# Early score maxima of ten query tiles: tile 0 and tiles 4 to 9 folded, and PSUM banks closed to maxima ahead of transposes and products

## The chip, the cores and the metric

One core of a Trainium2 chip runs the whole program in one launch. The metric is device time in microseconds (us), lower is better. TensorE is called PE, VectorE DVE, ScalarE ACT, GpSimd POOL and SyncE SP, as in the profile. L12 is line 12 of the kernel before, unless "of the change" stands beside it.

## The reference, cut to what matters

```python
for _ in range(2):                               # x is 2048 x 512
    n = layernorm(x)
    x = x + Cr @ (n @ Dr.T) - Ci @ (n @ Di.T)    # DFT over the sequence (2048) and over D (512)
    n = layernorm(x)
    q, k, v = n @ wq, n @ wk, n @ wv             # 32 query heads, one k and one v head, Dh = 16
    p = softmax(q @ k.T * 16 ** -0.5)            # for every head, 2048 x 2048
    x = x + (p @ v) @ wo
```

Everything is fp32 in and out. The softmax needs the maximum of each row of scores before the exponentials, and it is these maxima that the change moves.

## The kernel before, in words

Each of the two layers has a first phase (the Fourier part, then q, k and v) and a second phase (attention). The 2048 positions are 16 tiles of 128. Products run in fp32r, with operands split into a high and a low part, so a product of full accuracy is three matmuls. The DFT products from row 48 on, the scores and the maxima use 64 of PE's 128 rows (64*128 in the profile), and two of them run side by side on the two halves.

**First phase.** A loop over `n` from 0 to 127, called rows here, with 32 rows for each group of four tiles. A row of the first 112 multiplies one chunk of the DFT matrix into PSUM tiles `x` (L87 to L89 before row 48, L772 from then on); two rows share one turn of `z_rows`, and a place such as (2, 1) in the task table means quarter 1 of row 2 of a group. At the end of a group come the products with the hidden DFT (`y_rows`, L574), the residual sum (`y_out`, L556) and the statistics of the layer norm. While the next group's rows run, `prep_tasks` prepares the four tiles just finished: root and inverse of the variance (`ln_root`, `ln_inv`), the normalisation (`ln_apply`, L189), a PE transpose of each tile through bank `z` (`tr_tile`, L266), the k and v product (`kv`, L87 to L89 on a `y` bank), the transpose of v, and four q products (`q_mm`, on a `y` bank), whose results go to DRAM.

**Maxima.** A block is one PE matmul of a query tile's head pair with 512 keys (128 x 512 scores in one PSUM bank) and the DVE pass that takes its maximum. One tile has 16 pairs, two halves g and four key blocks, 128 blocks. Blocks of the first phase are *early*: the table `EARLY` lists tile, key block, the slot that holds the tile's queries, the row of its load, the row from which its blocks may be issued, the row by which they must be done, and the number of pairs. `pump` is called between the DFT products and issues a block when the kernel's own clocks (`clk`, a planner inside the recording code) say that a bank is free; `flush(n)`, at the start of row n, issues what is still left of the entries due, without waiting for a free bank and with nothing between. The banks are three `y` and one `z`.

An entry marked "f" is *folded*: the keys of blocks 0 and 1 are taken together. A first matmul with `kd` (block 0's keys less block 1's) gives a difference, ACT writes its Relu to `rel` or `kraw` (L463), a second matmul with `kz` gives block 1's scores, and one DVE pass (L468) adds the two and takes the maximum. So a folded pair of blocks is two matmuls, one ACT pass and one DVE pass; unfolded it is two matmuls and two DVE passes (L473). The `rel` and `kraw` tiles are one buffer for each half.

**Second phase.** 512 steps (16 tiles by 32 steps). A step is four score matmuls into two `x` tiles (L942; some of the last tile's into `y`, L935), two exponentials on ACT (L945, 128 x 1024), and the product of the step before last with v into bank `z` (L956, eight records of PE for a step). The remaining blocks (L398, L399) are issued by `more_max` in the order of the tiles, as many as `owed` allows: three to a step on average, four at most in one. A tile's blocks can be issued only when its queries are loaded (`o.loaded`): tile 13 takes the slot that tile 10's queries leave, so its load stands at step 0 of tile 11 and it counts as loaded at step 4 of tile 11. After each tile comes the output product with wo (12 matmuls).

## Time and profile before

| | us |
|---|---|
| median of 3 runs | 3548.38 (3547.25 to 3548.52) |
| the profiled execution | 3548.28 |
| its span in the profile | 3546.4 |
| first phase, layer 0 and layer 1 | about 0 to 633 and 1776 to 2395 |
| second phase, layer 0 and layer 1 | about 633 to 1776 and 2395 to 3546 |
| early blocks in a layer | 560 |
| blocks of `more_max` in a layer | 1472 |

The span begins with the first recorded instruction; 1.9 us of the execution lie outside it. Rows of a timeline are start, duration, engine, line, operation, written tile and read tiles. Matmuls overlap in the pipeline, so the distance between starts, not the duration, tells what one costs PE. An idle time stands in brackets with what ended it.

### The profile page before, as it was taken

The page shows a single profiled execution, that of the slowest core. Times are in us where ns is not written, and L with a number is a line of the kernel's source. Part 1 is how long each engine was busy: PE and PEld are TensorE (multiplying, and loading weights), DVE is VectorE, ACT ScalarE, POOL GpSimd, SP SyncE. Part 2 cuts the span into 40 slices and gives each one's busy share as a digit, 9 for nine tenths or more (in the row PEclk, how much of TensorE's full clock was granted, in tenths as well). Part 3 has the DMA queues.
Part 4 walks back from the last instruction along what each step waited for, and adds up shares of the span by engine and source line. Part 5 has one row for each costly group of instructions (what it writes and reads, how often), then busy time and mean ns, then how long its engine had stood idle before and what let it go on. Part 6 is the DMA issues. An engine that isn't in the chain of part 4 may idle for free.

```text
span 3546.4 us, 64237 instructions
## 1 busy us (share of the span) xinstructions
PE 3490.2 (98%) x24576; PEld 1884.6 (53%) x24576; DVE 2723.9 (77%) x4905; ACT 2499.3 (70%) x3204; POOL 818.7 (23%) x1212
## 2 busy tenths in 40 slices
PE   8999999999999999999999999999999999999999
PEld 6897879433333333333378978783333333333333
DVE  6267776888888888888432777768888888888883
ACT  4223733888888888888932237438888888888888
POOL 4244342211221122112213443322101110111011
PEclk9999999999999999999999999999999999999999
DMA  6445252311111100111144342423111111011100
GB/s 192 148 145 167 82 163 90 85 52 34 35 37 50 35 23 23 50 34 26 40 143 125 125 146 93 149 71 88 46 38 35 49 34 38 23 35 38 37 23 25
DMA packets 224899, 254.54 MB, mean 72 GB/s; under 512 B 52880, under 2 KB 174800, under 8 KB 217424
## 3 DMA queue, kind: packets, MB, share of 16 engines
q1 hardware_dynamic: 210384, 233.12, 21.5%
q0 software_dynamic: 14208, 17.33, 1.6%
q8 instruction: 193, 3.16, 0.4%
q14 instruction: 114, 0.93, 0.1%
HBM read 187.16 MB, written 65.27 MB: 71 GB/s over the span
## 4 chain that ended last, share of the span: by engine, by line
PE 93%; DVE 4%; ACT 2%; issue 1%; POOL 0%; DMA 0%; SPq 0%; ACTq 0%; DVEq 0%; POOLq 0%
PE z L956 29%; PE x L942 19%; PE y L398 13%; PE x L772 11%; PE y L87 3%; PE y L459 3%; PE y L88 2%; PE y L89 2%; PE x L574 2%; PE x L87 2%; PE x L89 2%; PE x L88 2%; DVE mxe L473 1%; DVE mxp L473 1%; PE z L459 1%
## 5 line engine op out<-in xcount | busy, mean ns | idle before, releaser
L945 ACT ACTIVATE slot<-x 128x1024 f32<-128x1024 f32 x2000 | 1946.2, 1024 | 284.2 <-PE x L942 272.3
L399 DVE TENSOR_REDUCE mxp<-y 128x1 f32<-128x512 f32 x2944 | 1849.8, 684 | 179.4 <-PE y L398 167.2
L956 PE MATMUL z<-slot,v 128*32 128x512 f32 x8192 | 1096.3, 605 | 1.6 <-DVE row L960 0.7
L942 PE MATMUL x<-slot,kz 64*128 64x512 f32 x2976 | 677.9, 451 | 0.7 <-DMA slot<-craw 0.4
L942 PEld LDWEIGHTS x<-slot,kz 64*128 64x128 f32 x2976 | 279.3, 184 | 742.9 <-ACT slot L945 686.4
L398 PE MATMUL y<-kz,slot 64*128 64x512 f32 x2176 | 581.2, 396 | 0.7 <-DVE mxp L399 0.4
L956 PEld LDWEIGHTS z<-slot,v 128*32 128x32 f32 x8192 | 163.4, 108 | 362.1 <-issue 331.1
L772 PE MATMUL x<-cl,xnh 64*128 64x512 f32 (+1 forms) x1536 | 352.4, 353 | 0.0
L772 PE MATMUL x<-ch,xnl 64*128 64x512 f32 (+1 forms) x1536 | 347.4, 358 | 1.1 <-ACT xnl L561 1.0
L772 PE MATMUL x<-ch,xnh 64*128 64x512 f32 (+1 forms) x1536 | 339.0, 358 | 6.5 <-DVE row L556 3.9
L398 PEld LDWEIGHTS y<-kz,slot 64*128 64x128 f32 x2176 | 277.5, 186 | 22.6 <-DVE mxp L399 10.4
L79 POOL TENSOR_TENSOR cl<-craw,ch 128x512 fp32r<-128x512 f32 x176 | 225.1, 1299 | 192.3 <-ACT ch L78 180.5
L78 ACT CAST ch<-craw 128x512 fp32r<-128x512 f32 x256 | 153.5, 622 | 156.2 <-PE x L89 81.7
L527 POOL DMA_DIRECT2D slot<-mt x224 | 111.5, 505 | 585.8 <-PE y L398 493.4
L459 PE MATMUL y<-kz,slot 64*128 64x512 f32 x602 | 232.7, 397 | 2.0 <-DVE kraw L304 1.0
L772 PEld LDWEIGHTS x<-ch,xnh 64*128 64x128 f32 x1536 | 210.0, 185 | 24.6 <-issue 6.6
L772 PEld LDWEIGHTS x<-ch,xnl 64*128 64x128 f32 x1536 | 214.3, 185 | 15.8 <-issue 4.5
L772 PEld LDWEIGHTS x<-cl,xnh 64*128 64x128 f32 x1536 | 217.3, 185 | 8.0
L997 POOL TENSOR_TENSOR row<-row,row 128x256 f32<-128x256 f32 x63 | 46.6, 739 | 700.1 <-DMA row<-rd 699.8
L473 DVE TENSOR_REDUCE mxe<-y 128x1 f32<-128x512 f32 x310 | 194.9, 680 | 14.0 <-PE y L459 14.0
L87 PE MATMUL x<-ch,xnh 128*128 128x512 f32 x384 | 154.3, 402 | 10.3 <-ACT ch L78 9.0
L89 PE MATMUL x<-ch,xnl 128*128 128x512 f32 x384 | 153.2, 399 | 2.0 <-POOL xnl L638 1.8
(197 smaller groups left out, 4173.8 us busy)
## 6 DMA issues: line engine op xcount, KB each, us to landing
craw<-ct_in SPq DMA_DIRECT2D x112, 512.0 KB
slot<-qd SPq DMA_DIRECT2D x44, 1024.0 KB
qd<-row SPq DMA_DIRECT2D x144, 128.0 KB
od<-row SPq DMA_DIRECT2D x252, 64.0 KB
row<-wqd SPq DMA_DIRECT2D x48, 256.0 KB
row<-x_in SPq DMA_DIRECT2D x32, 256.0 KB
mid<-row POOLq DMA_DIRECT2D x32, 256.0 KB, 2.4
craw<-ct_in SPq DMA_DIRECT2D x32, 256.0 KB
```

Source lines behind the costliest of these rows:

```text
L78: nc.scalar.copy(hi, raw)
L79: (eng or nc.vector).tensor_sub(lo, raw, f(hi))
L87: nc.tensor.matmul(ps_, ah, bh, start=start, stop=False)
L89: nc.tensor.matmul(ps_, al, bh, start=False, stop=stop)
L398: nc.tensor.matmul(pm, o.qT[i][gs, pr, :], kz[gs, c0:c0 + n], start=True, stop=True)
L399: nc.vector.reduce_max(to, pm, axis=AX.X)
L459: nc.tensor.matmul(pm, o.qT[i][gs, pr, :], k[gs, c0:c0 + 512], start=True, stop=True)
L473: nc.vector.reduce_max(to, pm, axis=AX.X)
L772: nc.tensor.matmul(z[d], a[gs, s, d * P:(d + 1) * P], b[gs, :], start=first and q < 2 and e == 0, stop=last and q > 1 and e == len(turns) - 1)
L942: nc.tensor.matmul(st["e"][:, g, :], kz[64 * g:64 * g + KR, c * P:(c + 1) * P], o.qT[i][64 * g:64 * g + KR, cp:cp + 4, :], start=True, sto ...
L945: nc.scalar.activation(ptiles[i, s_][:, 2 * w:2 * w + 2, :], st.pop("e"), AF.Exp, scale=DH ** -0.5)
L956: nc.tensor.matmul(a[32 * j:32 * j + 32, :], v1[:, c, :], pt[:, j, :], start=c == 0, stop=c == NT - 1)
```

## The change

The table of early blocks goes from 560 to 640 blocks a layer: tile 0's key blocks 0 and 1 are now folded, tiles 8 and 9 are new and folded, both due at row 119; (2, 1) and (1, 2) are gone. The preparation of four tiles starts earlier and in smaller steps. `hold` keeps maxima off bank `z` before each transpose; `keep` allocates the `y` bank of a coming k, v or q product ahead of it and lets only two more blocks through on `y`. No early block is issued between rows 64 and 70.8 and between 96 and 98.5. Of two tiles in `y_rows`, both sums now come before both statistics. The variance's eps goes through ACT's bias and POOL. At the end of the first phase four of the last eight maxima of tile 0 are issued one product earlier.

```diff
-    (1, 0, 2, 44, 49, 63, 16), (2, 0, 3, 44, 49, 63, 16), (3, 0, 8, 45, 49.5, 66, 16), (0, 0, 0, 64, 66.5, 79, 16),
-    (0, 1, 0, None, 71.5, 79, 16), (3, 1, 8, None, 71.5, 84, 16), (4, "f", 2, 77, 79.5, 95, 16), (5, "f", 3, 77, 79.5, 95, 16),
-    (6, "f", 8, 84, 87, 128, 16), (2, 1, 0, 96, 98, 111, 16), (1, 1, 1, 96, 98, 111, 16), (1, 2, 1, None, 103.5, 111, 8),
-    (7, "f", 2, 107, 109.5, 119, 16), (0, 2, 8, 101, 103.5, 128, 16),
+    (1, 0, 2, 43, 48, 63, 16), (2, 0, 3, 43, 48, 63, 16), (3, 0, 8, 44, 48, 66, 16), (0, "f", 0, 64, 70.8, 79, 16),
+    (3, 1, 8, None, 70.8, 84, 16), (4, "f", 2, 76, 78.5, 95, 16), (5, "f", 3, 76, 78.5, 95, 16), (6, "f", 8, 84, 87, 101, 16),
+    (7, "f", 0, 96, 98.5, 111, 16), (1, 1, 1, 96, 98.5, 111, 16), (0, 2, 8, 101, 103.5, 128, 16),
+    (8, "f", 2, 107, 109.5, 119, 16), (9, "f", 3, 107, 109.5, 119, 16),
...
-        nc.vector.tensor_scalar(v, mv[:, t0:t0 + n, 1], EPS, None, op0=ALU.add)
-        nc.scalar.activation(w, v, AF.Sqrt)
+        nc.scalar.activation(w, mv[:, t0:t0 + n, 1], AF.Sqrt, bias=eps)
+        nc.gpsimd.tensor_scalar(v, mv[:, t0:t0 + n, 1], EPS, None, op0=ALU.add)
...
+        def keep(after):
+            st["pk"], st["kept"] = bank("y"), 3
+            held("y", clk["pe"] + 1.4 + 2.8 + after)
...
-            tag = "z" if clk["z"] <= clk["y"][0] else "y"
+            tag = "z" if clk["z"] <= clk["y"][0] and not st["hold"] else "y"
...
+            if tag == "y" and st.get("kept") == 1:
+                return False
...
-                            y_out(4 * tb + w[e], y[:, e, :], x1[w[e]])
+                            y_add(4 * tb + w[e], y[:, e, :], x1[w[e]])
+                        for e in range(2):
+                            ln_stats(x1[w[e]], 4 * tb + w[e])
...
-            ts[0] = [alloc]
-            ts[1, 1] = [lambda: ln_inv(*st["root"])]
-            ts[2, 0], ts[2, 2] = [ap(0)], [ap(1)]
-            ts[2] = [lambda: tr(0)]
+            ts[0, 0] = [alloc, lambda: root_(0)]
+            ts[0, 2] = [lambda: ln_inv(*roots[0])]
+            ts[1, 1] = [ap(0), lambda: root_(2)]
+            ts[1, 2] = [ap(1), hold]
+            ts[1, 3] = [lambda: ln_inv(*roots[2])]
+            ts[2, 0] = [lambda: tr_(0)]
...
-            ts[6, 0] = [do_kv]
+            ts[4, 3] = [lambda: keep(2.6)]
+            ts[5, 1] = [do_kv]
...
-                ts[7 + g] = [lambda g=g: q_mm(tb, g, *st["xt"])]
+                ts[6 + g, 1] = [lambda: keep(0.9)]
+                ts[6 + g] = [lambda g=g: q_mm(tb, g, *st["xt"])]
...
-            q_rows(14, 0, *xt[1], lambda: None)
+            ticks = iter([0, 0, 0, 0, 1, 1, 1, 1])
+            q_rows(14, 0, *xt[1], lambda: take(mb, next(ticks)))
```

How the instructions move on PE is shown at three places, all in layer 1. The names are the PSUM bank that is written (`x`, `y`, `z`) and the operands; a row ending in x2 or x4 is that many equal matmuls.

The first transpose of the second group of tiles, before (L266, about row 67):

```order
L459 MATMUL y<-kz,slot_23056 128x512
L772 MATMUL x<-ch,xnh 128x512 x2
L459 MATMUL y<-kz,slot_23056 128x512
L772 MATMUL x<-cl,xnh 128x512 x2
L459 MATMUL z<-kz,slot_23056 128x512
L772 MATMUL x<-ch,xnl 128x512 x2
L266 MATMUL z<-ident,row_22480 128x128 x4
```

And of the change (L268 there, about row 66):

```order
L809 MATMUL x<-ch,xnh 128x512 x4
L809 MATMUL x<-cl,xnh 128x512 x2
L809 MATMUL x<-ch,xnl 128x512 x2
L268 MATMUL z<-ident,row_22653 128x128 x4
L809 MATMUL x<-ch,xnh 128x512 x2
```

Before, a block on bank `z` stands three matmuls ahead of the transpose that needs that bank; in the change no block stands anywhere near it.

The end of row 118, where `flush(119)` issues what is left of the entries due at row 119. Before (L459 are the blocks, `kd` the first matmul of a folded pair):

```order
L772 MATMUL x<-ch,xnl 128x256 x2
L459 MATMUL y<-kz,slot_26162 128x512
L459 MATMUL y<-kd,slot_26162 128x512 x2
L459 MATMUL z<-kz,slot_26162 128x512
L459 MATMUL y<-kz,slot_26162 128x512
L772 MATMUL x<-ch,xnl 128x256 x2
```

Of the change (L475), the beginning of the same place; the pattern of its last rows goes on, with no DFT product in it, until 70 blocks have been issued:

```order
L809 MATMUL x<-ch,xnl 128x256 x2
L475 MATMUL y<-kz,slot_26412 128x512 x2
L475 MATMUL y<-kd,slot_26412 128x512
L475 MATMUL z<-kd,slot_26412 128x512
L475 MATMUL y<-kz,slot_26412 128x512 x2
L475 MATMUL y<-kd,slot_26414 128x512
L475 MATMUL z<-kd,slot_26414 128x512
L475 MATMUL y<-kz,slot_26414 128x512 x2
L475 MATMUL y<-kd,slot_26414 128x512
```

So 5 blocks in a row became 70. Runs of the same kind stand at the ends of row 94 (9 blocks before, 21 now), of row 78 (none before, 9 now) and of row 110 (none before, 9 now, these unfolded).

Second phase, steps 334 and after. Before, every step to 487 carries three blocks (L398) among its scores (L942) and its products with v (L956):

```order
L942 MATMUL x<-slot_32910,kz 128x512 x2
L398 MATMUL y<-kz,slot_34495 128x512 x2
L942 MATMUL x<-slot_32910,kz 128x512 x2
L398 MATMUL y<-kz,slot_34495 128x512
L956 MATMUL z<-slot_36349,v_72 32x512 x4
```

Of the change, where steps without a block (the first three rows, step 356) end and step 357 begins (scores are L980, blocks L408, products with v L994):

```order
L980 MATMUL x<-slot_34217,kz 128x512 x4
L994 MATMUL z<-slot_37258,v_72 32x512 x4
L980 MATMUL x<-slot_34217,kz 128x512 x2
L408 MATMUL y<-kz,slot_37212 128x512 x2
L980 MATMUL x<-slot_34217,kz 128x512 x2
L408 MATMUL y<-kz,slot_37212 128x512 x2
L994 MATMUL z<-slot_37271,v_72 32x512 x4
L980 MATMUL x<-slot_34217,kz 128x512 x2
L408 MATMUL y<-kz,slot_37212 128x512 x2
```

In the change steps 0 to 333 carry three blocks as before, steps 334 to 356 none, steps 357 to 425 four, steps 426 to 461 three, and steps 462 to 511 none; before, steps 0 to 488 carry three and the rest none. 80 blocks fewer stand in this phase, and tile 13's, whose turn now comes at step 334, cannot be issued before step 357.

More of the change, by code (lines that the diff above doesn't have):

```diff
@@ L97, in fnet_mqa_kernel @@
     nc.gpsimd.memset(v1[:, :, DH:DH + 1], 1.0)
+    eps = sb.tile([P, 1], F32, name="eps")
+    nc.gpsimd.memset(eps, EPS)
     kone = sb.tile([P, 1], F32, name="kone")
@@ L271, in tr_tile, with kept @@
                 split_ps(v[0], xth, xtl)
+        def keep(after):
+            st["pk"], st["kept"] = bank("y"), 3
+            held("y", clk["pe"] + 1.4 + 2.8 + after)
+        def kept():
+            st["kept"] = 0
+            return st["pk"]
         def kv(t0, n, xth, xtl, vt=None, now=True):
-            pk = bank("y")[:, :n * P]
+            pk = (bank("y") if now else kept())[:, :n * P]
             spend(pe=2.9, act=1.2)
-            held("y", clk["pe"] + 2.5)
+            if now:
+                held("y", clk["pe"] + 2.5)
             for k in range(NK):
@@ L431, in make_layer @@
                 for e, ent in enumerate(EARLY)}
-        st["skew"], st["rel"], st["subs"] = 0, {}, []
+        st["skew"], st["rel"], st["subs"], st["hold"] = 0, {}, [], False
+        roots = {}
         def pump(n, only=None):
@@ L458, in issue @@
             pm = bank(tag)
+            if tag == "y" and st.get("kept"):
+                st["kept"] -= 1
+                assert st["kept"]
             nc.tensor.matmul(pm, o.qT[i][gs, pr, :], k[gs, c0:c0 + 512], start=True, stop=True)
@@ L686, in prep_tasks, with hold, tr_, root_ @@
[L686 removed]
+            def hold():
+                st["hold"] = True
+            def tr_(tt):
+                st["hold"] = False
+                tr(tt)
+            def root_(e):
+                roots[e] = ln_root(4 * tb + e, 2)
+            ts[0, 0] = [alloc, lambda: root_(0)]
[3 more added lines that the diff above has]
+            ts[1, 3] = [lambda: ln_inv(*roots[2])]
@@ new lines, in prep_tasks @@
+            ts[2, 0] = [lambda: tr_(0)]
+            ts[2, 1] = [hold]
+            ts[2, 2] = [ap(2)]
+            ts[2, 3] = [ap(3), lambda: tr_(1)]
+            ts[3, 0] = [hold]
+            ts[3, 1] = [lambda: tr_(2)]
+            ts[3, 2] = [hold]
+            ts[4, 0] = [lambda: tr_(3), lambda: [wq_load(g) for g in range(2)]]
+            ts[4, 3] = [lambda: keep(2.6)]
+            ts[5, 1] = [do_kv]
+            ts[6, 0] = [lambda: (kv_lo(4 * tb, 4), k_diff(tb) if tb < 2 else None), hold]
```

23 lines of the change are left out of this document (9 added, 14 removed).

## The prediction

> **What bounds the kernel now.** I read the page first, then the busy time by stage, then PE's own waits in the first phase.
>
> ```profile
> span 3546.4 us, 64237 instructions
> PE 3490.2 (98%) x24576; PEld 1884.6 (53%) x24576; DVE 2723.9 (77%) x4905; ACT 2499.3 (70%) x3204; POOL 818.7 (23%) x1212
> ```
>
> ```profile
> 1776.00:2395.00 619.00, 601.00 (x4493) 513.63 (x4491) 378.40 (x751) 242.56 (x502) 200.92 (x196) 1.00 0.38 122
> 2395.00:3546.00 1151.00, 1144.25 (x7811) 430.30 (x7810) 961.46 (x1626) 1000.03 (x1085) 137.87 (x258) 1.00 0.14 39
> ```
>
> The second fence is the first and the second phase of layer 1; the columns are the stretch, its length, and the busy time of PE, PEld, DVE, ACT and POOL. PE is the bound: in the first phase it is idle for 18 of 619 us while DVE works 378. But in the second phase DVE (961 of 1151) and ACT (1000) stand close behind, so what is taken from PE there is worth less than its PE time. Who holds PE up in layer 1's first phase:
>
> ```profile
> PE z L266 <- DVE mxp L473: 3.4, 3, 2.0
> PE z L266 <- DVE mxe L473: 2.7, 3, 1.4
> PE x L772 <- DVE row L556: 1.9, 2, 1.0
> PE y L87 <- DVE mxe L473: 1.4, 3, 0.5
> PE y L87 <- DVE mxp L473: 0.9, 2, 0.5
> PE y L459 <- DVE kraw L304: 0.5, 1, 0.5
> PE z L459 <- ACT v L314: 0.3, 1, 0.3
> ```
>
> Six transposes (L266) and five q products (L87) wait for a DVE maximum in the bank they need. That is what `hold` and `keep` go for. Each wait also costs a restart, which the timeline shows:
>
> ```profile
> 2040.32 0.61 PE L772 MATMUL x<-ch,xnl 64*128 64x512 f32 x2
> 2042.97 0.66 PE L266 MATMUL z<-ident,row 128*128 128x128 f32 x4 [2.04 <-DVE mxp L473]
> ```
>
> From the last start (two matmuls 0.23 apart, so 2040.55) the transposes were due at 2040.66 and started at 2042.97: 2.3 us lost, of which the idle time counts 2.04.
>
> **The change part by part**, all for one layer. Layer 0's first phase shows the same waits (its largest row stands here beside the 3.4 above), so everything is doubled at the end.
>
> ```profile
> PE z L266 <- DVE mxp L473: 3.6, 3, 2.3
> ```
>
> *The waits removed.* The rows on banks (all but the L556 row) sum to 9.2 us in 13 waits; with 0.3 us of restart each, 13.1. In the instruction order no block stands on `z` ahead of any transpose, and the `y` bank of a product is set apart early. What is late next is the layer norm's chain (root, inverse, four POOL steps, `ln_apply`), now started about 0.7 rows earlier. I keep a tenth for that: **-11.8** (bounds -8 and -13.1).
>
> *Both sums ahead of the statistics.* The L556 row is 1.9 us in two waits: the DFT products of a new group wait for the second tile's sum. A statistics pass (0.69) now no longer stands ahead of it, twice: **-1.4** (0 to -1.9).
>
> *Four maxima earlier at the end of the phase.*
>
> ```profile
> 2393.05 0.27 PE L533 MATMUL y<-ident,ms 128*32 128x128 f32 x1 [2.06 <-DVE ms L516]
> ```
>
> The transpose of the row maxima waits 2.06 us for DVE. With four of eight passes done one product earlier, the rest of the wait is DVE's short chain from the last maximum: **-1.4** (0 to -2.06).
>
> *80 more early blocks on PE.*
>
> ```profile
> 2039.86 0.39 PE L459 MATMUL y<-kz,slot 64*128 64x512 f32 x1
> 2040.08 0.40 PE L772 MATMUL x<-cl,xnh 64*128 64x512 f32 x2
> 2040.31 0.39 PE L459 MATMUL z<-kz,slot 64*128 64x512 f32 x1
> ```
>
> Half-array matmuls go in pairs, a pair every 0.23 us (2039.86, 2040.08, 2040.31): 0.117 each, and 80 x 0.117 = **+9.4**. The stage is bound by PE, so nothing hides it.
>
> *The forced runs.* This is the largest term. A run of blocks with nothing between is not paced by PE: it goes as fast as DVE and ACT empty the banks. Before has one such run, nine blocks at the end of row 94:
>
> ```profile
> 2170.29 1.05 PE L459 MATMUL y<-kd,slot 64*128 64x512 f32 x2
> 2171.12 0.50 PE L459 MATMUL z<-kz,slot 64*128 64x512 f32 x1
> 2171.73 0.49 PE L459 MATMUL y<-kz,slot 64*128 64x512 f32 x1
> 2171.81 1.11 PE L459 MATMUL y<-kd,slot 64*128 64x512 f32 x2
> ```
>
> ```profile
> 2170.36 0.69 DVE L468 CUSTOM_DVE_ANT_0 rel<-z,rel 128x512 f32<-128x512 f32 x1 [0.27 <-PE z L459]
> ...
> 2170.98 0.69 DVE L468 CUSTOM_DVE_ANT_0 kraw<-y,kraw 128x512 f32<-128x512 f32 x1
> ...
> 2171.79 0.69 DVE L468 CUSTOM_DVE_ANT_0 rel<-z,rel 128x512 f32<-128x512 f32 x1
> ...
> 2173.21 0.69 DVE L468 CUSTOM_DVE_ANT_0 rel<-z,rel 128x512 f32<-128x512 f32 x1
> ```
>
> ```profile
> 2171.16 0.60 ACT L463 ACTIVATE rel<-y 128x512 f32<-128x512 f32 x1 [0.29 <-DVE mxe L468]
> 2172.58 0.60 ACT L463 ACTIVATE rel<-y 128x512 f32<-128x512 f32 x1 [0.21 <-DVE mxe L468]
> ```
>
> The DVE pass on `rel` recurs every 1.42 us (2170.36, 2171.79, 2173.21). In that time go four blocks, two folded pairs. The reason stands in the last fence: `rel` is one buffer, so the next Relu waits for the DVE pass that reads it. Four blocks are 1.42 / 4 = 0.355 us each, against 0.117 of PE work: 0.238 lost on each. Behind the waiting matmuls on PE stand the next row's DFT products, and behind row 118's run also the hidden DFT of tiles 12 and 13; ACT, DVE, POOL and SP have nothing to do but serve the run.
>
> The instruction order has folded runs of 70 (row 118), 21 (row 94) and 9 (row 78) where before has 9 and 5: 86 more, x 0.238 = 20.5. The 9 unfolded blocks at row 110 go at DVE's pace, which two other rows show:
>
> ```profile
> L399 DVE TENSOR_REDUCE mxp<-y 128x1 f32<-128x512 f32 x2944 | 1849.8, 684 | 179.4 <-PE y L398 167.2
> ```
>
> ```profile
> 2393.79 3.68 DVE L399 TENSOR_REDUCE mxp<-y 128x1 f32<-128x512 f32 x6 [0.88 <-PE y L398]
> ```
>
> Six passes in 3.68 us, the last of 0.68: (3.68 - 0.68) / 5 = 0.60 from start to start. The last three can stay in their banks while PE goes on: 6 x 0.60 less 9 x 0.117 = 2.5. Together 23.0; each run may leave its last blocks in the banks too, so I take **+22** (16 to 26; the floor is two DVE passes 0.62 apart, 1.24 for four blocks).
>
> The Trainium skill ("ScalarE: Activation LUTs", Rules for kernel authors) says to use VectorE, not ScalarE, for relu and max, which speaks against folding with a Relu on ACT. These rows disagree: the Relu takes 0.60 beside DVE's 0.69. With both on DVE, four blocks would take 2 x (0.62 + 0.60) = 2.44 us by the rows and the runs 25 us a layer more; the sum goes by 1.42.
>
> *The second phase.* 80 blocks fewer, but placed worse. The step's price comes from counts over 800 us, and from the end of the kernel, where no block is left:
>
> ```profile
> 800.00:1600.00 800.00, 379.77 (x2856) 56.01 (x2848) 1.00 0.13 36
> 800.00:1600.00 800.00, 672.12 (x1071) 1.00 0.13 36
> 800.00:1600.00 800.00, 799.95 (x5499) 302.09 (x5491) 705.70 (x1238) 695.47 (x736) 161.32 (x337) 1.00 0.13 36
> 3517.11 1.12 PE L956 MATMUL z<-slot,v 128*32 128x512 f32 x8
> 3519.02 1.11 PE L956 MATMUL z<-slot,v 128*32 128x512 f32 x8
> ```
>
> The first row is L956 alone: 2856 / 8 = 357 steps, 2.24 us each with three blocks (second row, L399: 1071 / 357). The last two rows: 1.90 us without a block. DVE's other work is 705.70 - 672.12 = 33.6 us, 0.09 a step.
>
> Of the 512 steps, 489 carry three blocks before, and in the change 370 three, 69 four, and 73 none instead of 23. In numbers with fractions 118.7 steps of three become 69 of four and 49.7 of none. A step of four needs 4 x 0.60 + 0.09 = 2.49 us of DVE against 2.24 + 0.117 = 2.36 of PE, so DVE becomes the bound there. 69 x 2.49 + 49.7 x 1.90 - 118.7 x 2.24 = 171.8 + 94.4 - 265.9 = **+0.3**. So the 80 blocks that left this phase bring nothing: steps 334 to 356 starve because tile 13's queries are not there, and the blocks owed come back four to a step. Bounds: -9 if PE alone set the pace of four (2.36); +12 if four take 2.6 and the 41 empty steps that have only the two `x` tiles take 2.0.
>
> *At nothing:* the variance's eps on POOL (23% busy), and loads of queries a row or three quarters of a row earlier on SP, which stay as far ahead of their use as before. Uncovered, a late load costs PE a wait of a few us.
>
> **The sum**, a layer: -11.8 - 1.4 - 1.4 + 9.4 + 22 + 0.3 = +17.1; two layers +34. The profiled execution took 3548.28 (span 3546.4 and 1.9 outside), 0.1 from the median: **3582**.
>
> **The rivals.**
>
> *The clock drops in the long runs.* At the start of the second phase PE waits, and its granted clock falls; the column after the five busy times is the clock. The first row is the forced run at row 94:
>
> ```profile
> 2170.50:2173.50 3.00, 2.44 (x10) 1.20 (x10) 2.77 (x9) 2.47 (x6) 0.00 (x0) 1.00 0.53 175
> ...
> 2390.00:2395.00 5.00, 2.57 (x23) 1.44 (x19) 4.01 (x10) 2.99 (x6) 1.08 (x3) 1.00 0.00 0
> 2395.00:2400.00 5.00, 4.20 (x16) 2.31 (x16) 4.36 (x8) 2.27 (x3) 1.82 (x5) 0.63 0.36 77
> 2400.00:2410.00 10.00, 10.00 (x64) 3.55 (x62) 7.54 (x12) 7.53 (x9) 0.00 (x0) 0.84 0.20 43
> ```
>
> From the third row on that is 5 x 0.37 + 10 x 0.16 = 3.45 us of full clock lost. In a forced run PE works 4 x 0.117 of each 1.42 us, a third, for 25 us at row 118 and 7 at row 94. If that counts as idle, one or two such drops a layer: +7 to +14 in all, 3589 to 3596. The Trainium skill ("TensorE: Matmul & The Clock Gate", What's actually happening) has the clock halved after an idle window of about 3.4 us; the rows above agree in kind, and the 3 us of the run at row 94 show no drop. It does not say how a third of activity counts.
>
> *The transposes still wait*, for the layer norm's chain in place of the bank: `ln_apply` must be done 0.7 rows, some 2 us, earlier, and POOL's four small steps queue behind its splits of 1.3 us each.
>
> ```profile
> L79 POOL TENSOR_TENSOR cl<-craw,ch 128x512 fp32r<-128x512 f32 x176 | 225.1, 1299 | 192.3 <-ACT ch L78 180.5
> ```
>
> Then the 11.8 stay: 3582 + 24 = 3606.
>
> *PE sets the pace of four blocks*: the second phase gains 9 a layer: 3582 - 18 = 3564.
>
> *The forced runs drain at PE's pace* (the other side): if a run at row 118 cost only its 0.117 a block, the 22 would become -3.3 (what before loses in its own 14 forced blocks, 14 x 0.238), and a layer's sum 17.1 - 25.3 = -8.2: 3532, faster. Nothing in the profile speaks for it but the four banks, which let PE run ahead. It decides at about 0.19 us a block; the rows show 0.355, and the floor by DVE alone is 0.31.
>
> *That the closing of the banks does not happen* is excluded by the order; that it brings nothing is the second rival.
>
> **How the numbers follow.** Forecast 0.50, the clock 0.20, transposes still waiting 0.13, PE's pace 0.13, cheap runs 0.04. The forecast's own bounds: the runs from 16 (-12 in all) and the second phase to +12 (+23). The range reaches from PE's pace with somewhat cheaper runs, 3558, to the transposes' rival with a little of the clock, 3612. A measurement of this kernel can tell about 0.2%, 7 us, from no change; only cheap runs end below that, and a mixture of cheaper runs and PE's pace ends within it: faster 0.04, same 0.04, slower 0.92.
>
> **What would show it.** In the changed kernel's trace: PE's waits of L268 and of the q products near nothing; a run of 70 L475 blocks of about 25 us before row 119's products, with the folded DVE pass (L468 here) every 1.42 us on `rel`; a clock below 1.00 in the slices after it, or not; steps without L408 for about 44 us some 750 us into the second phase, then about 172 us of four blocks a step with DVE near 95%. I am wrong if the 70 blocks take under 14 us, or if the first phase is not longer than before.

## The result and the profile after

The changed kernel takes **3719.03 us** (median of 4 runs, 3717.83 to 3720.43) beside 3548.45 of the kernel before: ratio 1.0476, interval 1.0463 to 1.0488. The prediction said 3582 (3558 to 3612): slower was right, the size was a fifth of what came. The page after, its span and its busy times:

```profile
span 3716.5 us, 64865 instructions
PE 3614.5 (97%) x24576; PEld 1912.2 (51%) x24576; DVE 2614.4 (70%) x4892; ACT 2606.9 (70%) x3418; POOL 832.6 (22%) x1268
```

The span is 170.1 us longer, and PE's idle time is 102.0 (3716.5 - 3614.5) where it was 56.2. The rest, 124.3 us, is counted as busy although the number of matmuls is the same (24576), so at places they are longer in flight. By stage (stretch, length, busy PE, PEld, DVE, ACT, POOL, then the granted clock), the two layers one after the other:

```profile
0.00:675.00 675.00, 649.12 (x4563) 525.06 (x4563) 414.71 (x894) 311.46 (x631) 246.56 (x293) 0.96 0.41 132
675.00:1866.00 1191.00, 1160.75 (x7712) 432.78 (x7713) 919.71 (x1628) 999.59 (x1094) 240.92 (x499) 1.00 0.14 39
1866.00:2518.00 652.00, 641.57 (x4575) 519.41 (x4575) 372.20 (x831) 297.25 (x601) 207.53 (x219) 0.97 0.36 117
2518.00:3707.00 1189.00, 1158.80 (x7710) 432.24 (x7710) 905.52 (x1536) 997.88 (x1091) 137.62 (x259) 1.00 0.14 38
```

From the first score of a layer to its last product with v, the second phase is 48.8 us (layer 0) and 47.9 (layer 1) longer than before; the first phase 41.3 and 31.9. And the first phase runs at a granted clock of 0.96 and 0.97, where before has 1.00.

**Second phase.** It has 80 blocks fewer and DVE works less (905.52 against 961.46), yet it is longer. The 64 steps of four blocks from 360 to 423 of layer 1, by the products with v alone (512 records, eight a step), and below them all engines over the same time:

```profile
3325.10:3519.40 194.30, 68.18 (x512) 10.07 (x512) 1.00 0.10 29
...
3325.10:3519.40 194.30, 173.70 (x1049) 69.03 (x1048) 163.49 (x275) 125.67 (x133) 15.27 (x28) 1.00 0.10 29
```

That is 194.3 / 64 = 3.036 us a step; before, the same 64 steps with three blocks take 143.1, 2.236 each. And no engine is full: DVE works 163.5 of 194.3, 84% where the prediction had near 95%, and ACT 125.7. One such step, in the timeline of PE and DVE:

```profile
3440.99 0.50 PE L980 MATMUL x<-slot,kz 64*128 64x512 f32 x2
3441.33 0.40 PE L408 MATMUL y<-kz,slot 64*128 64x512 f32 x2
3441.56 0.39 PE L980 MATMUL x<-slot,kz 64*128 64x512 f32 x2
3441.75 2.48 DVE L409 TENSOR_REDUCE mxp<-y 128x1 f32<-128x512 f32 x4 [0.45 <-PE y L408]
3441.79 0.40 PE L408 MATMUL y<-kz,slot 64*128 64x512 f32 x1
3442.50 0.50 PE L408 MATMUL y<-kz,slot 64*128 64x512 f32 x1 [0.31 <-DVE mxp L409]
3442.93 1.06 PE L994 MATMUL z<-slot,v 128*32 128x512 f32 x8
3443.92 0.50 PE L980 MATMUL x<-slot,kz 64*128 64x512 f32 x2
```

Read it from the two rows with a bracket. There are three `y` banks. Blocks one, two and three take them at 3441.33 to 3441.79; the fourth needs the first block's bank, which DVE starts to read at 3441.75 and needs 0.6 to 0.7 us for. So the fourth starts at 3442.50, 1.17 us after the first, and behind it in PE's order stand the product with v (0.43 later, at 3442.93; it takes 0.99) and the next scores. The step is 0.34 + 1.17 + 0.43 + 0.99 = 2.93 us (the mean of 3.036 also holds the output products of two tiles). DVE then waits in its turn (0.45) for the next step's first block. PE waits for DVE and DVE for PE in each step: a round trip, in which both have slack. With three blocks each bank comes back a whole step later, and nobody waits.

**The forced run at row 118.** Its first and last matmul start 28.4 us apart in layer 0 and 29.0 in layer 1. Folded DVE passes (L484) on `rel`, early in the run and in its middle, layer 1:

```profile
2409.49 0.69 DVE L484 CUSTOM_DVE_ANT_0 rel<-y,rel 128x512 f32<-128x512 f32 x1
...
2410.91 0.69 DVE L484 CUSTOM_DVE_ANT_0 rel<-y,rel 128x512 f32<-128x512 f32 x1
...
2426.21 0.69 DVE L484 CUSTOM_DVE_ANT_0 rel<-y,rel 128x512 f32<-128x512 f32 x1 [0.32 <-ACT rel L479]
...
2427.90 0.69 DVE L484 CUSTOM_DVE_ANT_0 rel<-y,rel 128x512 f32<-128x512 f32 x1
```

At first they come every 1.42 us, as in the run of nine before; then every 1.69. Two block matmuls of the same two moments, and the clock (the number behind POOL's busy time) ahead of the run, at its start, in it and behind it:

```profile
2410.12 0.49 PE L475 MATMUL z<-kd,slot 64*128 64x512 f32 x1
...
2426.23 0.79 PE L475 MATMUL y<-kd,slot 64*128 64x512 f32 x1
```

```profile
2405.00:2410.00 5.00, 4.89 (x61) 4.15 (x57) 4.58 (x11) 3.82 (x9) 2.56 (x2) 1.00 0.01 3
2410.00:2415.00 5.00, 4.28 (x14) 2.19 (x13) 4.13 (x14) 3.73 (x8) 0.00 (x0) 0.77 0.32 107
2415.00:2420.00 5.00, 5.00 (x13) 2.42 (x12) 4.08 (x13) 3.58 (x6) 0.00 (x0) 0.50 0.00 0
...
2440.00:2445.00 5.00, 5.00 (x54) 4.40 (x53) 4.55 (x10) 1.04 (x3) 0.00 (x0) 1.00 0.01 3
```

PE's busy time does not show it: 5.00 of 5.00 with 13 matmuls, since one in flight counts as busy. The run goes from 2408.8 to 2437.8; some 4 us into it the clock falls to 0.50, and it stays there until 2 us behind it. A matmul then takes 0.79 us instead of 0.49, and 0.30 more of it stands in each round of ACT and DVE, about the 0.27 by which the period grew. In layer 0 the two change together: the passes on `rel` come every 1.42 us up to 568.85, the first matmul of 0.79 us starts at 569.53, where the clock falls, and the next pass on `rel` comes after 1.70, at 570.55. In layer 1 the first longer round (1.74 us) ends just before the fall, so the order is not as clean there.

**The waits that were to go** (PE, layer 1's first phase; before had 3.4, 2.7, 1.4 and 0.9 us at transposes and q products):

```profile
PE z L268 <- DVE mxp L489: 1.7, 1, 1.7
...
PE y L475 <- ACT rel L479: 0.6, 3, 0.2
PE y L475 <- DVE mxe L484: 0.5, 1, 0.5
...
PE z L475 <- ACT kraw L479: 0.2, 1, 0.2
```

The closing works where it is done: the six waits of transposes and the five of q products are gone, and the blocks themselves wait 1.3 us in five waits. But the 1.7 us are a new wait. It is the transpose of tile 13, which did not wait before, and a block on `z` (the first row) stands two matmuls ahead of it:

```profile
2468.27 0.40 PE L475 MATMUL z<-kz,slot 64*128 64x512 f32 x1
...
2470.45 0.66 PE L268 MATMUL z<-ident,row 128*128 128x128 f32 x4 [1.67 <-DVE mxp L489]
```

`hold` is called in `prep_tasks` alone, which prepares tiles 0 to 11; the transposes of tiles 12 and 13, at rows 122 and 123, stand outside it, and so they are not protected, other than "The change" says. Layer 0 has the same wait (1.7 us). In layer 0 one more transpose waits, at about row 70, and for the layer norm:

```profile
PE z L268 <- DVE row L191: 3.9, 1, 3.9
```

### The profile page after: what moved, and what is told of

Read it like the earlier page. It is cut to its first block, busy times and chain, and to the rows that moved or that the text cites. A ratio compares the mean times of both kernels' runs of the same rounds, so it can differ in the third digit from the quotient of the medians.

```text
span 3716.5 us, 64865 instructions
## 1 busy us (share of the span) xinstructions
PE 3614.5 (97%) x24576; PEld 1912.2 (51%) x24576; DVE 2614.4 (70%) x4892; ACT 2606.9 (70%) x3418; POOL 832.6 (22%) x1268
## 4 chain that ended last, share of the span: by engine, by line
PE 85%; DVE 6%; ACT 4%; issue 3%; POOL 1%; DMA 0%; SPq 0%; ACTq 0%; POOLq 0%; DVEq 0%
PE z L994 26%; PE x L980 16%; PE y L408 12%; PE x L809 10%; PE y L475 3%; PE y L87 3%; DVE mxp L409 3%; PE y L88 2%; ACT slot L983 2%; PE y L89 2%; PE x L87 2%; PE x L89 2%; PE x L88 2%; PE z L475 2%; DVE mxe L489 1%
## 5 line engine op out<-in xcount | busy, mean ns | idle before, releaser
L409 DVE TENSOR_REDUCE mxp<-y 128x1 f32<-128x512 f32 x2784 | 1744.8, 683 | 203.3 <-PE y L408 192.7
L994 PE MATMUL z<-slot,v 128*32 128x512 f32 x8192 | 1096.1, 605 | 4.7 <-DVE row L998 3.4
L980 PE MATMUL x<-slot,kz 64*128 64x512 f32 x2944 | 673.8, 455 | 13.3 <-ACT slot L983 11.5
L408 PE MATMUL y<-kz,slot 64*128 64x512 f32 x2272 | 638.5, 402 | 45.5 <-DVE mxp L409 45.3
L980 PEld LDWEIGHTS x<-slot,kz 64*128 64x128 f32 x2944 | 276.4, 184 | 747.6 <-ACT slot L983 673.1
L408 PEld LDWEIGHTS y<-kz,slot 64*128 64x128 f32 x2272 | 295.9, 186 | 130.2 <-DVE mxp L409 112.2
L994 PEld LDWEIGHTS z<-slot,v 128*32 128x32 f32 x8192 | 164.0, 108 | 341.0 <-issue 311.2
L475 PE MATMUL y<-kz,slot 64*128 64x512 f32 x594 | 261.3, 450 | 3.2 <-ACT rel L479 1.2
L484 DVE CUSTOM_DVE_ANT_0 rel<-y,rel 128x512 f32<-128x512 f32 x194 | 134.1, 691 | 77.4 <-PE y L475 53.9
L479 ACT ACTIVATE rel<-y 128x512 f32<-128x512 f32 x204 | 122.3, 599 | 84.2 <-PE y L475 39.9
L489 DVE TENSOR_REDUCE mxe<-y 128x1 f32<-128x512 f32 x238 | 149.6, 679 | 20.0 <-PE y L475 19.9
```

The costliest lines, as they stand in the source:

```text
L408: nc.tensor.matmul(pm, o.qT[i][gs, pr, :], kz[gs, c0:c0 + n], start=True, stop=True)
L409: nc.vector.reduce_max(to, pm, axis=AX.X)
L475: nc.tensor.matmul(pm, o.qT[i][gs, pr, :], k[gs, c0:c0 + 512], start=True, stop=True)
L489: nc.vector.reduce_max(to, pm, axis=AX.X)
L980: nc.tensor.matmul(st["e"][:, g, :], kz[64 * g:64 * g + KR, c * P:(c + 1) * P], o.qT[i][64 * g:64 * g + KR, cp:cp + 4, :], start=True, sto ...
L994: nc.tensor.matmul(a[32 * j:32 * j + 32, :], v1[:, c, :], pt[:, j, :], start=c == 0, stop=c == NT - 1)
```

## The experiments

Each ran against the kernel before on the same chip. There the kernel before took 3550.16 to 3550.45, some 2 us more than beside the changed kernel, so a difference from the changed kernel's 3719.03 can be wrong by about 2 us. The theory: the 97 us of the second phase are mostly the fourth block's wait in its 138 steps, and most of the rest is the forced run at row 118, with the clock that it costs. The rivals: the second phase is long for another reason (DVE, ACT, late queries); the closing itself costs something.

**1. The closing alone.** The changed code with the table of before:

```diff
-    (1, 0, 2, 43, 48, 63, 16), (2, 0, 3, 43, 48, 63, 16), (3, 0, 8, 44, 48, 66, 16), (0, "f", 0, 64, 70.8, 79, 16),
...
-    (8, "f", 2, 107, 109.5, 119, 16), (9, "f", 3, 107, 109.5, 119, 16),
+    (1, 0, 2, 44, 49, 63, 16), (2, 0, 3, 44, 49, 63, 16), (3, 0, 8, 45, 49.5, 66, 16), (0, 0, 0, 64, 66.5, 79, 16),
...
+    (7, "f", 2, 107, 109.5, 119, 16), (0, 2, 8, 101, 103.5, 128, 16),
```

> All of the change but its table: the 560 early blocks of before with the new preparation and the banks closed. Forced runs of 15 and 12 blocks a layer in the order, second phase as before. Theory (the closing works as priced, the loss lies in the table): 11.8 + 1.4 + 1.4 us gained a layer, about 3 lost in the longer forced runs, some 6 lost in layer 0 to the one transpose that waits for the layer norm: 3530 to 3538. Rival (the earlier preparation only swaps one wait for another): 3548 or more.

Measured: 3549.88 (3547.85 to 3552.23), ratio 0.9999 (0.9990 to 1.0009). No cost, but no gain: the rival's number. The eleven waits are gone from its list as well, and tile 13's 1.7 us has come. A part of the gain is lost in and behind its forced runs, which are 15 and 12 blocks now instead of 9 and 5, because blocks that may not go ahead of a transpose are left over at the due row. Two windows at the run at row 94, in it and behind it, first of this kernel, then of the kernel before:

```profile
2170.00:2173.00 3.00, 2.33 (x10) 1.08 (x10) 2.83 (x9) 2.54 (x5) 0.00 (x0) 0.98 0.51 175
2173.00:2176.00 3.00, 3.00 (x14) 2.10 (x15) 1.81 (x6) 2.03 (x4) 0.00 (x0) 0.50 0.00 0
```

```profile
2170.00:2173.00 3.00, 2.63 (x12) 1.19 (x9) 2.62 (x9) 2.46 (x6) 0.20 (x1) 1.00 0.53 175
2173.00:2176.00 3.00, 2.81 (x25) 2.17 (x26) 2.63 (x9) 2.35 (x5) 0.00 (x0) 1.00 0.00 0
```

Nine blocks in a row leave the clock at 1.00, fifteen halve it. It goes by the time and not by the number: in the traces of all kernels with single matmuls, forced runs of up to 3.0 us leave the clock at 1.00, and those from 3.9 us on halve it, also the nine unfolded blocks at row 110 of the changed kernel, which take 4.7 us. Summed over one-us windows, this kernel loses 5.1 us of full clock in layer 1's first phase, in three drops of 1.7 us each, two behind these runs and one behind tile 13's wait; the kernel before loses none. Its first phases are 637.5 and 619.8 us, against 633.8 and 620.4. In layer 1 the closing and the two smaller terms should have given back 14.6 us, and 0.6 came; the longer runs (3.5 us by their length), the lost clock (5.1 at most) and the new wait (1.7) explain some 10 of the 14, and the rest is open.

**2. At most three blocks in a step**, otherwise the changed kernel:

```diff
+                to = o.done + 3
...
-                        if owed(n) >= 1:
+                        if owed(n) >= 1 and o.done < to:
```

> The change with at most three blocks in a step of the second phase; steps 334 to 356 stay empty, steps 357 to 484 carry three, the rest none. Theory (69 steps with four blocks cost 3.04 us each): the second phase of a layer falls from 1190 us to about 1135, so 3719 - 110 = 3609, with the first phase unchanged at 652 and 665 to 670. Rival (the starved steps and the two x tiles cost the time, not the steps of four): the second phase stays above 1175, 3690 or more.

Measured: 3614.66 (3612.90 to 3615.19), ratio 1.0182 (1.0167 to 1.0198): 104 us less than the changed kernel, all of it in the second phase, which is now 1138.1 and 1137.5 us, 3.7 less than before. The late queries and the empty steps from 334 to 356 are the same as in the changed kernel, so they are not the cause; whether it is DVE's amount of work is left to number 6. Sixty-four of its steps, all with three blocks, take 143.0 us, 2.235 each, and PE is never idle:

```profile
3325.10:3468.10 143.00, 143.00 (x988) 53.91 (x992) 125.04 (x211) 124.95 (x133) 15.51 (x28) 1.00 0.12 31
```

**3. Without tile 9's entry** (576 blocks; forced runs of 9, 21, 9 and 6 blocks):

```diff
-    (8, "f", 2, 107, 109.5, 119, 16), (9, "f", 3, 107, 109.5, 119, 16),
+    (8, "f", 2, 107, 109.5, 119, 16),
```

> The change without tile 9's early blocks: 576 early blocks a layer, the forced run at row 118 falls from 70 to 6, and the second phase has five steps of four and three starved ones. Theory (the forced run and the steps of four are the loss): the first phase falls by about 28 + 7 us a layer, the second to about 1140, in all 3719 - 71 - 98 = 3550. Rival (the runs at rows 78, 94 and 110 and the earlier preparation weigh as much): 3600 or more.

Measured: 3566.36 (3564.90 to 3567.21), ratio 1.0047 (1.0032 to 1.0062). So one entry, 64 of the 640 blocks, is worth 152.7 us of the 170.6. Without it the steps from 360 to 424 are 2.236 again and the second phase is 1142.9 and 1143.3; the first is 644.8 and 624.4, 30.3 and 27.9 below the changed kernel. It is still 11.0 and 4.0 above before: 16 us more than I had expected. The runs of 21 and 9 and layer 0's row 70 (number 10) are still there and can make that up, but this run does not take them apart.

**4. The fourth block elsewhere in the step.** Two of the four between the halves of the product with v:

```diff
+                if j == 1:
+                    between()
...
-                for j, m in ((g, 0), (1 - g, 2), (2 + g, 0), (3 - g, 2)):
+                for j, m in ((g, 0), (1 - g, 2), (2 + g, 0), (3 - g, 0 if four else 2)):
```

> The change with its four blocks of a step placed two after the first pair of scores and two in the middle of the product with v, instead of four within a quarter of the step. Number of blocks, banks and steps are as in the change. Theory (three y banks and PE's order make a round trip PE, DVE, PE of 2.9 to 3.0 us when all four come close together): a step of four falls to 2.5 us, DVE's own pace, 37 us a layer, 3645. Rival (four blocks in a step simply cost 3.04, by contention of DVE or ACT): 3719.

Measured: 3769.03 (3767.81 to 3770.54), ratio 1.0620 (1.0602 to 1.0637): neither. The step became 3.39 us, for a reason that neither theory had:

```profile
3483.19 1.05 PE L994 MATMUL z<-slot,v 128*32 128x512 f32 x4
3484.17 0.50 PE L408 MATMUL y<-kz,slot 64*128 64x512 f32 x2
3484.60 1.05 PE L994 MATMUL z<-slot,v 128*32 128x512 f32 x4
```

Half of the product (four records) takes 0.98 us (3483.19 to 3484.17), as long as the whole of it took in the step shown above (eight records, 0.99): the four matmuls of 128 x 32 go side by side, and cutting them apart pays twice. The experiment tells nothing of the banks; the next one was made for that.

**5. The fourth block behind the product**, which stays whole:

```diff
+                if four:
+                    more_max()
...
-                for j, m in ((g, 0), (1 - g, 2), (2 + g, 0), (3 - g, 2)):
+                for j, m in ((g, 0), (1 - g, 2), (2 + g, 0), (3 - g, 1 if four else 2)):
```

> The change, with the fourth block of a step of the second phase placed behind the product with v instead of behind the third block; all else as in the change. Theory (with three y banks the fourth block waits for the first one's DVE pass, and PE's whole queue with it): a step of four falls from 3.04 to about 2.5 us, since the product with v now covers the wait: 37 us a layer less, 3645. Rival (four blocks a step cost 3.04 by themselves): 3719.

Measured: 3688.52 (3687.60 to 3690.16), ratio 1.0388 (1.0372 to 1.0403). A step of 2.81 instead of 3.04: two fifths of what I expected (74 us, and 30.5 came). The order of a step now begins with a block, but its last block still needs the first one's bank:

```profile
3420.55 1.06 PE L994 MATMUL z<-slot,v 128*32 128x512 f32 x8
3421.54 0.50 PE L408 MATMUL y<-kz,slot 64*128 64x512 f32 x1
...
3421.88 0.63 PE L408 MATMUL y<-kz,slot 64*128 64x512 f32 x2
...
3422.82 0.50 PE L408 MATMUL y<-kz,slot 64*128 64x512 f32 x1
3423.25 1.07 PE L994 MATMUL z<-slot,v 128*32 128x512 f32 x8
```

From the first block to the last are 1.28 us, a little more than the 1.17 of the changed kernel; but the first stands 0.33 earlier in the step, right behind the product, so the step is 2.70.

**6. A shorter pass on DVE.** The test that does not touch PE's order at all:

```diff
-            nc.vector.reduce_max(to, pm, axis=AX.X)
+            nc.vector.reduce_max(to, pm[:, :256] if n == 512 else pm, axis=AX.X)
...
-                nc.scalar.activation(ptiles[i, s_][:, 2 * w:2 * w + 2, :], st.pop("e"), AF.Exp, scale=DH ** -0.5)
+                nc.scalar.activation(ptiles[i, s_][:, 2 * w:2 * w + 2, :], st.pop("e"), AF.Exp, scale=DH ** -0.5 / 16)
```

> The changed kernel, but each maximum of the second phase reads only the first 256 of its 512 scores on DVE (the matmul still makes all 512), and the exponent is scaled down by 16 so that nothing overflows; both change the output. A maximum then takes about 0.42 us instead of 0.68 (an estimate: 256 elements fewer at the 1.04 ns an element that 128x512 passes of 0.53 show). Theory (the fourth block of a step waits until DVE has emptied the first block's bank): a step of four falls from 3.035 us to between 2.35 and 2.55, and a step of three, which PE sets, stays at 2.24; 138 steps x 0.5 to 0.7 = 69 to 95 us less than the changed kernel, 3624 to 3650. Rival (the step of four is long by PE's own order or by ACT): it stays at 3.0 or more and the time at 3712 to 3720.

Measured: 3677.50 (3677.32 to 3679.70), ratio 1.0357 (1.0340 to 1.0374). The step of three stays at 2.24, the step of four falls to 2.77: 0.27 us, which is one DVE pass's saving (0.68 to 0.42), not four. That is what a round trip with exactly one pass in it gives. My 2.35 to 2.55 was too low because the trip is not gone, only shorter:

```profile
3420.83 0.40 PE L408 MATMUL y<-kz,slot 64*128 64x512 f32 x2
...
3421.27 1.43 DVE L409 TENSOR_REDUCE mxp<-y 128x1 f32<-128x256 f32 x4 [1.25 <-PE y L408]
3421.30 0.94 PE L408 MATMUL y<-kz,slot 64*128 64x512 f32 x2
3421.74 0.18 PEld L408 LDWEIGHTS y<-kz,slot 64*128 64x128 f32 x1 [0.49 <-DVE mxp L409]
3422.17 1.07 PE L994 MATMUL z<-slot,v 128*32 128x512 f32 x8
```

First block 3420.83, fourth 3421.74 (its weights): 0.91 instead of 1.17. DVE is idle 1.25 us in each step, so its amount of work cannot be the bound; the step still is not PE's 2.36.

**7. The forced matmuls twice.** Each matmul of a forced run is issued a second time into the same bank, so that PE is busier and nothing else changes:

```diff
-            nc.tensor.matmul(pm, o.qT[i][gs, pr, :], k[gs, c0:c0 + 512], start=True, stop=True)
+            for _ in range(2 if force else 1):
+                nc.tensor.matmul(pm, o.qT[i][gs, pr, :], k[gs, c0:c0 + 512], start=True, stop=True)
```

> The change, with every matmul of a forced run issued twice into the same bank (the second overwrites the first with the same values), so that PE is busy for twice as much of the run. Theory (PE working a third of the time lets the clock fall to 0.50, and at half clock a group of four blocks takes 1.69 us instead of 1.42): the clock stays near 1.00, the run at row 118 falls from about 29 us to 25 or 26 although PE does more, and the half-speed stretches behind the runs go: 3 to 6 us less a layer, 3707 to 3713. Rival (the clock is a bystander, the group is slow for another reason): the run stays at 29 us or grows by up to 70 x 0.117 = 8 us: 3719 to 3735.

Measured: 3713.56 (3712.84 to 3714.68), ratio 1.0458 (1.0440 to 1.0475), half a us above the expected time, and not by the expected way. Two windows inside its run at row 118:

```profile
2410.00:2415.00 5.00, 5.00 (x26) 2.91 (x25) 3.97 (x14) 3.70 (x7) 0.00 (x0) 1.00 0.00 0
2420.00:2425.00 5.00, 5.00 (x26) 3.09 (x27) 3.94 (x12) 3.51 (x7) 0.00 (x0) 1.00 0.02 5
```

With 26 matmuls in 5 us instead of 13 the clock stays at 1.00, so PE's activity is what decides it. The 5.5 us gained (7.5, each beside its own kernel before) are mostly behind the runs, where the next rows no longer start at half clock. The two first phases are 3.6 and 1.8 us shorter than the changed kernel's, although behind the runs some 7 and 5 us of full clock are no longer lost: a us of lost clock costs less than a us. The run itself is as long as before (28.4 and 28.8 us, a period of 1.63): the second matmul put back into each round trip about what the clock had taken. So that the slow clock makes the period 1.69 rests on the rows under the result, and this run does not show it by itself.

**8 and 9. Two tables with 560 blocks.** The changed code with a folded table (and the clearing copies of the query memory, `qd_zero`, at rows 48 to 59):

```diff
-    (3, 1, 8, None, 70.8, 84, 16), (4, "f", 2, 76, 78.5, 95, 16), (5, "f", 3, 76, 78.5, 95, 16), (6, "f", 8, 84, 87, 101, 16),
+    (3, 1, 8, None, 70.8, 84, 8), (4, "f", 2, 76, 78.5, 95, 16), (5, "f", 3, 76, 78.5, 95, 16), (6, "f", 8, 84, 87, 101, 16),
...
-    (8, "f", 2, 107, 109.5, 119, 16), (9, "f", 3, 107, 109.5, 119, 16),
+    (8, "f", 2, 107, 109.5, 119, 16),
...
-                    add(2 * t + 4 if t < 4 else 3 * t + 38, lambda t=t: qd_zero(t))
+                    add(2 * t + 4 if t < 4 else t + 44, lambda t=t: qd_zero(t))
```

> The change's code with 560 early blocks chosen from its table (no tile 9, eight pairs of (3, 1)): forced runs of 9, 9, 9 and 6, second phase as before; and in layer 0 POOL's copies of zero rows, which stand at rows 50 to 83, at rows 48 to 59. Theory (the closing gives back about 13 us a layer, and the forced runs and the layer norm's wait behind POOL take them): layer 1's first phase 616 to 620 against 620.4, and layer 0's without its 6 us at row 70, 629 to 633 against 633.8: 3535 to 3546. Rival (the early preparation itself costs): 3550 or more, with layer 0's 6 us still there.

Measured: 3548.86 (3545.52 to 3549.50), ratio 0.9994 (0.9984 to 1.0003): between the two forecasts. Layer 1's first phase is 619.2 us, as expected, layer 0's 633.9, no shorter than before. And such a table in the code of before:

```diff
-    (1, 0, 2, 44, 49, 63, 16), (2, 0, 3, 44, 49, 63, 16), (3, 0, 8, 45, 49.5, 66, 16), (0, 0, 0, 64, 66.5, 79, 16),
-    (0, 1, 0, None, 71.5, 79, 16), (3, 1, 8, None, 71.5, 84, 16), (4, "f", 2, 77, 79.5, 95, 16), (5, "f", 3, 77, 79.5, 95, 16),
-    (6, "f", 8, 84, 87, 128, 16), (2, 1, 0, 96, 98, 111, 16), (1, 1, 1, 96, 98, 111, 16), (1, 2, 1, None, 103.5, 111, 8),
-    (7, "f", 2, 107, 109.5, 119, 16), (0, 2, 8, 101, 103.5, 128, 16),
+    (1, 0, 2, 44, 49, 63, 16), (2, 0, 3, 44, 49, 63, 16), (3, 0, 8, 45, 49.5, 66, 16), (0, "f", 0, 64, 71.5, 79, 16),
+    (3, 1, 8, None, 71.5, 84, 8), (4, "f", 2, 77, 79.5, 95, 16), (5, "f", 3, 77, 79.5, 95, 16), (6, "f", 8, 84, 87, 101, 16),
+    (7, "f", 0, 96, 98, 111, 16), (1, 1, 1, 96, 98, 111, 16), (0, 2, 8, 101, 103.5, 128, 16),
+    (8, "f", 2, 108, 110.5, 119, 16),
```

> The kernel before with 560 early blocks of the change's folded kind and none of the new preparation: tile 0 folded, tiles 4 to 8 folded, eight pairs of (3, 1), no (0, 1), (2, 1), (1, 2). Same number of blocks on PE, 48 DVE passes fewer a layer. Theory (transposes wait for the banks, not for DVE's total): the waits stay, and forced runs of 6, 9 and 9 add about 4 us a layer: 3550 to 3558. Rival (DVE's total is the limit of the first phase, folding frees it): 3530 to 3540.

Measured: 3552.72 (3550.78 to 3554.64), ratio 1.0005 (0.9996 to 1.0015). Folding other tiles and closing the banks each move nothing, alone or together, as long as the number of blocks stays: the closing's gain that I still expected of the first of them did not come.

**10 and 11. The clearing copies earlier.** Their one line, as in number 8, in the changed kernel and in number 1.

> The changed kernel with the copies that clear the query memory (qd_zero, one each for 16 tiles) at rows 48 to 59 instead of one in every third row from 50 to 83. Theory (in layer 0 a normalisation pass on DVE takes 9.7 us at row 70, because POOL works without a pause beside it, with those copies' DMA issues in POOL's order): the stretch of layer 0 from row 70 on falls from 16.2 to about 9.5 us and the time by 6 to 7, to 3712 to 3713. Rival (the pass is slow for another reason, such as the splits of the DFT matrix alone): no difference, 3717 to 3720.

Measured: 3713.09 (3711.37 to 3715.19), ratio 1.0458 (1.0442 to 1.0473), 5.9 less than the changed kernel (7.8, each beside its own kernel before); the first phase of layer 0 is 667.1 instead of 675.1. The two normalisations behind the second `rs` in layer 0, and POOL beside them, first in the changed kernel:

```profile
276.61 1.19 POOL L121 DMA_DIRECT2D qd<-qd  x2
276.64 10.14 DVE L191 TENSOR_SCALAR row<-row,mv,rs 128x512 f32<-128x512 f32 x2 [1.15 <-POOL rs L160]
277.82 2.53 POOL L79 TENSOR_TENSOR cl<-craw,ch 128x512 fp32r<-128x512 f32 x2
...
280.31 3.75 POOL L84 TENSOR_TENSOR slot<-row,slot 128x512 fp32r<-128x512 f32 x3
...
284.02 2.47 POOL L79 TENSOR_TENSOR cl<-craw,ch 128x512 fp32r<-128x512 f32 x2
```

and then with the copies moved:

```profile
276.71 2.71 POOL L79 TENSOR_TENSOR cl<-craw,ch 128x512 fp32r<-128x512 f32 x2
276.80 2.91 DVE L191 TENSOR_SCALAR row<-row,mv,rs 128x512 f32<-128x512 f32 x2 [1.15 <-POOL rs L160]
```

Two passes of DVE take 10.14 us in the first and 2.91 in the second. The copies set off the 3.9 us wait on PE (and half a clock for 7 us behind it); why one pass then stays stuck through seven POOL instructions, while the next kernel's POOL works without a pause as well, is open.

> The changed kernel's code with the early blocks of the kernel before (560 a layer) and the clearing copies at rows 48 to 59. With the table of before alone it took 3549.9 and its layer 0 lost 2.3 us at row 70. Theory: 2 to 3 us less, 3546.5 to 3548, so at most 0.1% faster than before. Rival: nothing, 3549 to 3551.

Measured: 3547.15 (3544.48 to 3548.42), ratio 0.9990 (0.9981 to 1.0000): the fastest of all, by 0.1% at most, which is less than 0.2% and so no gain to rely on. No version that was tried beats the kernel before by more than that.

## Why the prediction was wrong, point by point

For each layer, forecast and measured:

| | forecast | measured, layer 0 and 1 |
|---|---|---|
| second phase | +0.3 | +48.8, +47.9 |
| first phase | +16.8 | +41.3, +31.9 |
| of it: all forced runs, beyond 0.117 a block | +22 | +28.5, +28.8 |
| in them: length of the 70 blocks at row 118 (before: 5) | 24.9 | 28.8, 29.4 |
| of it: full clock lost behind the runs | 0 | at most 8.6, 5.4 |
| of it: normalisation stuck at row 70 | 0 | +8.0, 0 |

- **The step of four failed**, and with it the forecast. It was priced as "4 x 0.60 + 0.09 = 2.49 us of DVE", the larger of two engines' work. It took 3.036, and 69 x (3.036 - 2.49) = 37.7 us. The price assumed that banks never run out; with three banks and four blocks, the fourth waits in PE's queue, ahead of everything else, for one DVE pass (numbers 2, 5 and 6). The bound of 2.6 did not hold it either. I had the order of a step before me, with two times two blocks between the scores and three `y` banks in the text, and did not run through it once.
- **Steps without a block** were priced at 1.90 by two steps at the kernel's end. Counted between the products with v that open the steps, the 73 empty ones of the changed kernel's layer 1 take 148.0 us (steps 334 to 356 46.7, steps 462 to 511 101.3) and the 23 of before 46.8, so the 50 more take 2.03 each: 49.7 x 0.13 = 6.5 us. The bound of 2.0 for such steps was right. The steps of three that went had taken 2.20 and not 2.24 (261.3 us for 119), another 5 us. With the step of four that is some 49 us, beside +48.8 and +47.9. The starving of steps 334 to 356 and its place were right.
- **The forced runs**: their mechanism and place were right (70 blocks, ACT and DVE in turn, DVE every 1.42 us on `rel` at first), their price was too low: 28.5 and 28.8 us against +22 and its bound of 26, since the run at row 118 is 3.9 and 4.5 us longer than forecast and the others are longer too (7.7 and 7.5 us at row 94, 2.8 at row 78, 4.7 at row 110). And "one or two such drops a layer", the rival at 0.20, came true: the clock at 0.50 for nearly the whole run. I had put the rival's price at +7 to +14 in all. In the run at row 118 it is those 3.9 and 4.5, as far as the clock sets the period. Behind the runs, by one-us windows, about 5 us of full clock are lost in layer 1 (of 18.8 in its first phase, 12.6 lie inside the run at row 118, where PE has time to spare, and about 1 in that at row 94) and 8.6 in layer 0: some 22 in all, if each of them counted. Number 7 says that they do not: with the clock kept up, the first phases fell by 3.6 and 1.8.
- **The waits removed**: the mechanism was right, 11.8 was too much. The eleven waits of transposes and q products are gone (8.4 us). But that "no block stands on `z` ahead of any transpose" was wrong for tile 13, which waits 1.7 us in each layer. The blocks' own waits were 1.2 us (the list left out two of 0.2) and are 1.3. So 15 waits of 9.6 us became six of 3.0, and with restarts of 0.3 some 9 us are gone. Longer forced runs and the clock take them back for the most part (number 1, where the closing alone gives 0 and not the 11.5 a layer that my terms add up to, 14.6 less 3.1 for longer runs). What was to be late next, the layer norm's chain, was late once: at row 70 of layer 0, and not by its 0.7 rows but by POOL and the copies (+8.0, number 10).
- **The 80 blocks**: 0.117 each in the first phase was taken over; what leaves the second phase is worth less than that (1138.1 with no step of four, -3.7 for 80 blocks, 0.05 each). So early blocks lose here even when nothing waits.
- **Both sums ahead of the statistics, and the maxima at the phase's end**: right. Neither the 1.9 us for L556 nor the transpose's 2.1 is in the list any more.
- With these terms up to 2 us a layer of the first phase's excess are not accounted for if the lost clock is counted in full, and about 5 if it costs what number 7 gave back.

The Trainium skill ("TensorE: Matmul & The Clock Gate", What's actually happening) gives a free-running window of 3413 ns after which an idle TensorE is halved. The runs agree in the quantum: each drop costs 1.7 us of full clock, or a multiple (3.4 at the 21 blocks of row 94 of the changed kernel), and half of 3.41 is 1.71. Its section "A second HAM failure mode: psum-queue depth-cycling" says that in another kernel TensorE, idle briefly and often while it went round the banks, swung between half and full speed. The run at row 118 agrees in the fall (14 matmuls at 0.117 in 5 us, a third of PE's time, and no idle gap over 0.2 us), but the clock did not swing there: it stayed at 0.50 for 27.3 us.

## What to carry to other kernels

Where work goes round between two engines through a few buffers, count the buffers against what one turn of the loop needs before any sum of busy times: at one more than there are, the round trip's latency is paid in every turn, and everything queued behind it waits too. A burst that another engine paces also costs what comes after it, if it slows the clock. And work moved off a stage is worth only what that stage's own bound gives back, here 0.05 us a block (number 2) against 0.117 paid.

## What the runs showed of the hardware

- The clock was granted 0.50 during a run whose matmuls took a third of PE's time, with no idle gap over 0.2 us. Forced runs of up to 3.0 us (5 to 9 folded blocks) did not bring it down, and runs of 3.9 us and more did (11 folded blocks and more, or nine unfolded). Issuing each matmul twice kept it at 1.00 in the runs at rows 94 and 118.
- A normalisation pass of 128x512 on DVE, 0.54 us elsewhere, took 9.7 us beside POOL's splits, from a DMA issue of POOL on, and about 1.5 us in a kernel without that issue. The Trainium skill ("SBUF — State Buffer", Who interferes with whom) says that a pass which uses both of DVE's ports, as this operation can, and a POOL instruction block each other for one whole instruction, whichever starts first. No row shows the ports; the 1.5 us would agree (0.54 and the rest of one POOL instruction of 1.3), the 9.7 us do not: seven POOL instructions passed.
- Four products with v on four column groups of 32 take as long as two of them: 0.99 and 0.98 us.
